# Gate logits on VectorE and ScalarE, and memory numerators with their denominators in one matmul per block, in a gated memory-attention and GLU kernel

## The chip, the cores and the metric

The kernel runs on one core of one Trainium2 chip. Its time is the device time of one execution in microseconds (us); a median of several runs is quoted. The profiled span, from the first to the last recorded instruction, is 1.6 to 1.9 us shorter than the measured time of the same execution.

PE is TensorE's matmul stream, PEld its weight loads, PEq its sequencer, DVE is VectorE, ACT is ScalarE, POOL is GpSimd and SP is SyncE. "The Trainium skill" is the set of notes on the chip that this text cites by page and section. PSUM is the memory into which matmuls write, and an eviction is the instruction that takes a result out of it.

## The reference

It mixes a segmented attention with a compressive memory (32 heads of 16 dimensions, 4 segments of 512 tokens) and a gated GLU, token by token. Cut to what matters here:

```python
x = A_x                                              # 1 x 2048 x 512, bfloat16
g = sigmoid((x * gate_w).sum(-1, keepdims=True))     # one gate logit per token
a = A_ref(x, ...)                                    # attention with memory
b = ((gelu(x @ w_gate)) * (x @ w_up)) @ w_down       # 512 -> 1792 -> 512
return g * a + (1 - g) * b

# inside A_ref, for each segment s of 512 tokens:
    p = softmax(qs @ ks.T * scale + mask);  a_dot = p @ vs
    pq = phi(qs)
    num = einsum('bhld,bhde->bhle', pq, M)           # memory numerators
    den = einsum('bhld,bhd->bhl', pq, z) + 1e-6      # memory denominators
    o = gb * (num / den) + (1 - gb) * a_dot          # gb = sigmoid(beta), per head
    M = M + phi(ks).T @ vs;  z = z + phi(ks).sum(l)
```

## The kernel before

The program declares tasks (a few instructions for one engine, with what they read and write). A scheduler with estimated durations and a table of biases then puts every engine's tasks into one fixed order. So the order of each engine's queue is decided when the program is built, and an instruction that is late holds up all that stand behind it on its engine.

The three parts of attention that matter: score matmuls on tiles of 32 rows fill all of one score buffer (`XALL`, 2048 columns of PSUM); one exponential of 2048 columns on ScalarE empties it; the next scores may start only then, because there is only one such buffer. TensorE uses the time of the exponential for full 128x128 matmuls (projections, GLU).

```python
# scores, then one exponential over the whole score buffer (72 times)
for (lhs, rhs, c0, ncol, rd) in steps:
    for g in range(4):
        instrs.append(Instr(lambda e, ...: e.matmul(X[g][:, c0:c0 + ncol], lhs(32 * g), rhs(32 * g),
                            start=True, stop=True, tile_position=(32 * g, 0)), rd, [("X", g)], ...))
...
exp_task(s, f"exp{s}_{t}{name}", [Instr(lambda e: e.activation(
    dst[:], XALL[:, :].rearrange("p (g c) -> p g c", g=4), ACTF.Exp, scale=ATT_SCALE),
    [("X", g) for g in range(4)], [key], act_t(2048))], after=after)
```

The gate logits and the denominators are groups of sixteen very narrow matmuls on TensorE:

```python
# gate logits of one segment: 16 matmuls of ONE column, weights are 128x128 blocks of x
pieces(f"gate{s}", gg, [mm(gg, lambda tile=tile: gg.f32()[:, tile:tile + 1],
                           xT[x3][:, kb, tile * 128:(tile + 1) * 128], gatew[:, kb:kb + 1],
                           [*xk(s, kb), ("w", "gatew")], kb == 0, kb == 3, 1)
                        for tile in range(4) for kb in range(4)], 16)
...
# denominators of one segment (s > 0): 16 matmuls of EIGHT columns
pieces(f"den{s}", gd, [mm(gd, lambda qt=qt, t=t: gd.f32()[:, 32 * qt + 8 * t:32 * qt + 8 * t + 8],
                          phq[:, t, qt * 128:(qt + 1) * 128], MZbd[:, t, 16:136:17], ...)
                       for qt in range(4) for t in range(4)], 16)
# VectorE: + eps, reciprocal, * (gate x head mix), 128 columns each
...
for qt in range(4):       # numerators: 4 matmuls of 128 columns, with the SAME weights phq as above
    pieces(f"num{s}_{qt}", gn, [mm(gn, ..., phq[:, t, qt * 128:(qt + 1) * 128],
                                   MZbd[:, t, :]...[:, :, 0:16], ..., 128) for t in range(4)], 4)
    task(f"nump{s}_{qt}", DVE, [ ... tensor_tensor(otok[...], gn.f32()[...], ndsc[...], ALU.mult) ], grp=gn)
```

The softmax here doesn't subtract the row's maximum and nothing guards it: scores larger than these inputs give would overflow.

## Time and profile before

| | before |
|---|---|
| median of 3 runs | 270.14 us (270.02 to 270.32) |
| profiled span | 268.6 us |
| PE busy | 259.8 us (97%) |
| ScalarE busy | 211.9 us (79%), of which 72 exponentials 135.0 |
| VectorE busy | 185.8 us (69%) |
| recorded matmuls / weight loads | 3075 / 3118 |

From the page of the profile of the kernel before: the busy time of each engine, and the chain of work that ended last, followed back in time, as shares of the span.

```profile
span 268.6 us, 7243 instructions
## 1 busy us (share of the span) xinstructions
PE 259.8 (97%) x3075; PEld 122.3 (46%) x3118; DVE 185.8 (69%) x333; ACT 211.9 (79%) x179; POOL 95.2 (35%) x223
...
PE 95%; issue 2%; ACT 2%; DVE 0%; ACTq 0%
```

These are the waits of PE and of PEld in the kernel before (who waited, for whom, us in total, how often, the longest); the weight load belongs to the matmul that follows it.

```profile
engine line waited for: us in total, times, longest us
...
PEld psXALL L775 <- ACT pt L782: 22.9, 54, 0.4
...
PE psW L439 <- issue: 3.8, 24, 0.2
PEld psXALL L775 <- ACT ptl L782: 2.5, 6, 0.4
...
PE psW L524 <- DVE pt L503: 1.1, 1, 1.1
```

"issue" is idle time for which the profile shows no releaser; the 24 holes of 0.16 us are missing matmuls, as the experiments will show.

The Trainium skill ("ScalarE: Activation LUTs", "What ACT_TABLE_LOAD costs") gives an activation with immediate operands as 186 ns + 0.833 ns per column; an estimate from it for 2048 columns is 1892 ns. This trace has 1875 ns, so it agrees within 1%.

The removed groups in the grouped view of the kernel before (busy us, mean ns of one; these durations are pipeline latencies and overlap, so they are not what a matmul costs the stream):

```profile
L439 PE MATMUL psW<-mzbd,phq 128*128 128x128 bf16 x48 | 4.2, 223 | 0.0
L439 PE MATMUL psW<-gatew,xT 128*128 128x1 bf16 x64 | 2.2, 163 | 0.0
L439 PE MATMUL psW<-mzbd,phq 128*128 128x8 bf16 x48 | 1.7, 176 | 0.0
```

### The profile page before, as it was taken

How to read it: one execution, taken by the hardware profiler on the slowest of the kernel's cores; microseconds unless marked ns; L12 is line 12 of the kernel's file. 1: busy time of each engine (PE TensorE's matmuls, PEld its weight loads, DVE VectorE, ACT ScalarE, POOL GpSimd, SP SyncE). 2: the span in 40 equal slices, each digit the busy share in tenths (PEclk: the TensorE clock that was granted, in tenths of full speed). 3: DMA queues.
4: the chain of work that ended last, by engine and by line, in shares of the span. 5: the costliest groups of instructions: out<-in, count | busy, mean ns of one | idle time of the engine just before them, and what ended most of it. 6: DMA issues, size and time to landing. Idle time of an engine off the chain costs nothing.

```text
span 268.6 us, 7243 instructions
## 1 busy us (share of the span) xinstructions
PE 259.8 (97%) x3075; PEld 122.3 (46%) x3118; DVE 185.8 (69%) x333; ACT 211.9 (79%) x179; POOL 95.2 (35%) x223
## 2 busy tenths in 40 slices
PE   8999999999999999999999999999999999999996
PEld 5445344444445444544444444444354434444354
DVE  1678997988978659798525988798851677353451
ACT  3889987999998898889768898877777767677602
POOL 8328853542002843252201574252300252352300
PEclk9999999999999999999999999999999999999999
DMA  6998991000304510102011310213020000000002
GB/s 194 203 323 185 362 212 22 4 0 2 81 2 98 81 42 0 45 20 42 20 24 39 60 23 1 58 27 82 1 44 0 2 0 2 20 22 32 9 2 78
DMA packets 32056, 16.53 MB, mean 62 GB/s; under 512 B 21400, under 2 KB 32024, under 8 KB 32024
## 3 DMA queue, kind: packets, MB, share of 16 engines
q1 hardware_dynamic: 31736, 15.81, 25.4%
q8 instruction: 24, 0.39, 0.6%
q10 hardware_dynamic: 288, 0.26, 0.3%
q14 instruction: 8, 0.07, 0.1%
HBM read 8.14 MB, written 2.10 MB: 38 GB/s over the span
## 4 chain that ended last, share of the span: by engine, by line
PE 95%; issue 2%; ACT 2%; DVE 0%; ACTq 0%
PE psW L439 75%; PE psXALL L775 9%; PE psW L824 6%; PE psXALL L439 1%; PE psW L832 1%; PE psW L524 1%; PE psW L742 1%; ACT pt L782 1%; PE psXALL L533 1%; ACT hT L909 1%; ACT L909 0%; ACT ost L958 0%; DVE pt L503 0%; ACTq L336 0%
## 5 line engine op out<-in xcount | busy, mean ns | idle before, releaser
L782 ACT ACTIVATE pt<-psXALL 128x2048 bf16<-128x2048 f32 x64 | 120.0, 1875 | 27.4 <-PE psXALL L775 24.3
L786 POOL TENSOR_SCALAR_AFFINE_SELECT pt<-pt 128x256 bf16<-128x256 bf16 x128 | 55.4, 434 | 139.3 <-ACT pt L782 132.7
L439 PE MATMUL psW<-xT,wu 128*128 128x512 bf16 x214 | 51.0, 379 | 1.1 <-issue 0.8
L439 PE MATMUL psW<-xT,wg 128*128 128x512 bf16 x213 | 50.3, 380 | 1.4 <-issue 1.1
L439 PE MATMUL psW<-wd,hT 128*128 128x512 bf16 x201 | 49.9, 380 | 1.1 <-issue 1.0
L930 DVE TENSOR_TENSOR hT<-psW,hT 128x512 bf16<-128x512 f32 x56 | 37.5, 685 | 15.6 <-PE psW L439 15.4
L839 DVE STREAM_TRANSPOSE tb<-psW 128x512 f32<-128x512 f32 x32 | 21.1, 696 | 18.9 <-PE psW L832 18.8
L439 PEld LDWEIGHTS psW<-xT,wu 128*128 128x128 bf16 x224 | 20.6, 98 | 24.8 <-issue 1.7
L439 PEld LDWEIGHTS psW<-xT,wg 128*128 128x128 bf16 x224 | 20.3, 98 | 24.5 <-issue 1.7
L439 PEld LDWEIGHTS psW<-wd,hT 128*128 128x128 bf16 x210 | 18.8, 98 | 22.7 <-issue 2.7
L775 PE MATMUL psXALL<-qT,kpad 32*128 32x320 bf16 (+3 forms) x512 | 25.4, 273 | 0.0
L909 ACT ACTIVATE hT<-psW 128x512 bf16<-128x512 f32 x28 | 16.4, 597 | 7.5 <-PE psW L439 7.5
L786 POOL TENSOR_SCALAR_AFFINE_SELECT ptl<-ptl 128x2048 bf16<-128x2048 bf16 x8 | 17.1, 2138 | 8.7 <-ACT ptl L782 8.4
L775 PEld LDWEIGHTS psXALL<-qT,kpad 32*128 32x128 bf16 x512 | 7.6, 92 | 26.5 <-ACT pt L782 20.8
L824 PE MATMUL psW<-pt,vaug 128*17 128x192 bf16 (+3 forms) x512 | 18.9, 273 | 0.0
L782 ACT ACTIVATE ptl<-psXALL 128x2048 bf16<-128x2048 f32 x8 | 15.0, 1876 | 2.8 <-PE psXALL L775 2.7
L439 PE MATMUL psW<-xT,wk 128*128 128x512 bf16 (+1 forms) x66 | 15.8, 381 | 0.2 <-issue 0.2
L691 POOL COPY exsT<-exs 32x4 f32<-32x4 f32 x64 | 14.6, 228 | 3.7
L439 PE MATMUL psW<-wo,oT 128*128 128x512 bf16 x55 | 14.8, 380 | 0.7 <-issue 0.5
L439 PE MATMUL psW<-xT,wq 128*128 128x512 bf16 x60 | 14.9, 380 | 0.5 <-issue 0.3
L456 DVE CAST hT<-psW 128x512 bf16<-128x512 f32 x21 | 14.0, 679 | 1.7 <-PE psW L439 1.5
L439 PE MATMUL psW<-wv,xT 128*128 128x512 bf16 x62 | 15.1, 380 | 0.1
(94 smaller groups left out, 285.5 us busy)
## 6 DMA issues: line engine op xcount, KB each, us to landing
out_dram<-ost SPq DMA_DIRECT2D x15, 128.0 KB, 1.7
wg<-in_B_w_gate_dram SPq DMA_DIRECT2D x2, 896.0 KB, 6.4
wu<-in_B_w_up_dram SPq DMA_DIRECT2D x2, 896.0 KB, 6.8
wd<-in_B_w_down_dram SPq DMA_DIRECT2D x1, 1792.0 KB, 13.1
vlow<-vaug SPq DMA_DIRECT2D x8, 136.0 KB, 3.5
wv<-in_A_wv_dram SPq DMA_DIRECT2D x1, 512.0 KB, 6.2
wo<-in_A_wo_dram SPq DMA_DIRECT2D x1, 512.0 KB, 14.0
wk<-in_A_wk_dram SPq DMA_DIRECT2D x1, 384.0 KB, 4.8
```

The source lines that it names most:

```text
L439: return Instr(lambda e: e.matmul(view(), lhsT, rhs, start=first, stop=last), reads=reads, writes=[fkey if fkey is not None else g.key], e ...
L456: alts[DVE] = [Instr(lambda e: e.tensor_copy(dst(), src()), reads=reads, writes=writes, est=dve_t(n))]
L524: task(f"warm{i}", PE, [Instr(lambda e, gw=gw, n=n: e.matmul(gw.f32()[:, 0:128 * n].rearrange("p (o c) -> p o c", c=128), warm[:, 0:128], ...
L533: task(f"x0t{i}_{u}", PE, [Instr(lambda e, k=k, a=a, u=u, i=i, src=src: e.transpose(src[:, k, a * 128:(a + 1) * 128], xin[:, 2 * u + a, (2 ...
L691: cross = task(f"exsT{s}", POOL, [Instr(lambda e, g=g, c=c: e.tensor_copy(exsT[sl][32 * g:32 * g + 32, c:16:4], exs[32 * c:32 * c + 32, s4 ...
L775: instrs.append(Instr(lambda e, g=g, lhs=lhs, rhs=rhs, c0=c0, ncol=ncol: e.matmul(X[g][:, c0:c0 + ncol], lhs(32 * g), rhs(32 * g), start=T ...
L782: prev_exp[0] = exp_task(s, f"exp{s}_{t}{name}", [Instr(lambda e: e.activation(dst[:], XALL[:, :].rearrange("p (g c) -> p g c", g=4), ACTF ...
L786: task(f"msk{s}_{t}{name}", POOL, [Instr(lambda e, view=view, pat=pat, base=base: e.affine_select(out=view, in_=view, compare_op=ALU.is_ge ...
L824: instrs.append(Instr(lambda e, t=t, q=q, kb=kb, slot=slot, c0=c0: e.matmul(gp.f32()[32 * q:32 * q + 17, 128 * kb + 64:512], Vaug[sl][:, k ...
L839: task(f"pvt{s}_{t}_{j}", DVE, [Instr(lambda e: e.transpose(Tb[:, j, :], gp.f32()[:, :]), [gp.key], [("Tb", j)], dve_t(512))], grp=gp)
L909: lambda e, g=g, ft=ft, s=s: e.activation(hT[s % 2][:, ft, :], g.f32()[:, :], ACTF.Gelu_apprx_tanh),
L930: task(f"Um{s}_{ft}", DVE, [Instr(lambda e, g=g, ft=ft: e.tensor_tensor(hT[sl][:, ft, :], g.f32()[:, :], hT[sl][:, ft, :], ALU.mult), [g.k ...
```

## The change

The intent is to take 113 small matmuls off TensorE. The gate logits become an elementwise multiply of token-major x with a broadcast gate vector on VectorE, and row sums on VectorE or ScalarE; for three of the four segments x is loaded once more for it, 1.5 MB in all. The denominators ride along as the 17th column of each head in the numerators' matmuls, 136 columns in place of 128. The head mix is folded into the memory matrix on GpSimd and VectorE, and the eviction of numerators becomes a short chain (add eps and scale, reciprocal, multiply) per group of 2 or 3 blocks. The warm-up matmuls read a constant. Because tasks changed, the table of biases was tuned again, which re-orders all queues.

```diff
-    task("gwt", PE, [ ... e.transpose(gwg.bf()[:, 0:4], gwrow[:, :], ident[0:4, 0:4]) ... ])
...
-        pieces(f"gate{s}", gg, [mm(gg, ..., xT[...], gatew[:, kb:kb + 1], ..., 1)
-                                for tile in range(4) for kb in range(4)], 16)
+        task(f"gmul{s}", DVE, [Instr(lambda e: e.tensor_tensor(
+            xt[:, 0:4, :], xt[:, 0:4, :], gwb[:]...to_broadcast([P, 4, D]), ALU.mult), ...)])
+        for a in range(4):
+            S.add(Task(f"gsum{s}_{a}", {
+                ACT: [... e.activation(xt[:, a, :], xt[:, a, :], ACTF.Copy, accum_out=glog[...]) ...],
+                DVE: [... e.tensor_reduce(glog[...], xt[:, a, :], AXX, ALU.add) ...]}))
...
-            pieces(f"den{s}", gd, [mm(gd, ..., MZbd[:, t, 16:136:17], ..., 8) ...], 16)
-            for qt in range(4):
-                pieces(f"num{s}_{qt}", gn, [mm(gn, ..., MZbd[...][:, :, 0:16], ..., 128) ...], 4)
+            for pr in range(2):
+                for k in range(3):
+                    blocks = [(2 * pr + k, t) for t in range(3)] if k < 2 else [(2 * pr, 3), (2 * pr + 1, 3)]
+                    pieces(f"num{s}_{pr}{k}", gn, [mm(gn, ..., gn.f32()[:, 136 * i:136 * i + 136],
+                           phq[:, t, qt * 128:(qt + 1) * 128], MZbd[:, t, :], ..., 136) ...], 3)
+                    ins = [ tensor_scalar(nd, den column, EPS, exr, add, mult), reciprocal(nd), tensor_tensor(otok, num, nd) ]
...
-                bdmask[32 * c:32 * c + 32]...to_broadcast([32, 4, 34]),          # block-diagonal mask
+                gbd[32 * c:32 * c + 32]...                                     # mask times head mix
...
 BIAS = { ... all values changed ... }
```

## The prediction

> **What bounds it now.** TensorE. The page of the profile puts PE at 259.8 of 268.6 us (97%), and the chain of waits is 95% PE. The list of waits names almost nothing that PE waited for: 1.06 us at the start (a VectorE memset of the warm-up operand), about 2.9 us of tail after the last matmul, and scattered "issue" gaps of 0.16 us that fit missing matmul records. VectorE (185.8 us) and ScalarE (211.9 us) have slack on average, but little between 25 and 75 us, where the table by stretches shows both at 8 to 10 of 10 us. So time is saved only in PE's stream, and lost where VectorE or ScalarE then returns a PSUM bank late.
>
> **What PE loses and gains** (start-to-start times in the trace):
> - The gate logits: 4 groups of 16 one-column matmuls. Within a group they start 25 ns apart, and the next full matmul starts 0.62 us after the first of the group: 4 x 0.62 = 2.5 us. The 25 ns is the issue floor that the Trainium skill gives ("TensorE: Matmul & The Clock Gate", "Wait — 56ns, not 53.3ns?"); this trace agrees.
> - The gate-vector transpose: 0.1 us.
> - The denominators: 3 groups of 16 eight-column matmuls, 27 ns apart, 0.64 us to the next full matmul (0.53 in one): 1.8 us.
> - The numerators go from 48 matmuls of 128 columns (59 ns apart) to 48 of 136, estimated at 62.6 ns: +0.16 us. They stand in 15 runs instead of 7. Leaving such a run cost 275 ns instead of 59 in about half the cases: estimated +0.9 us.
>
> Net about -3.3 us. Switches between full-array and tiled matmuls are equal in number; all other matmuls are the same.
>
> **What the others gain** (estimates from like instructions). VectorE: four 2048-element multiplies (about 1.25 us, from 0.70 for 1024), about 11 row sums (0.69), 18 smaller denominator chains in place of 3 large ones. About +18 us in all, so near 203 us busy. ScalarE: about 5 row sums of 0.6 us. About 5 us of VectorE's increase falls before the first up-projection (now at 67.8 us), where VectorE would be about 95% busy: I allow 0.5 us of new PE waits, there or around the numerator evictions. GpSimd's extra work and the 1.5 MB of extra x loads are off the path.
>
> **Start.** The warm-up no longer waits for the memset: about 0.15 us earlier, but it has 128 more cold columns (0.11 us), and then the x tiles and first key weights set the pace (landed 3.3 to 7.0 us, used within 0.1 to 0.5 us). Worth 0.1 us at most. The tail stays.
>
> **Prediction.** 270.1 - 3.3 - 0.1 + 0.5 = 267.2 us (-1.1%), 8 in 10 within 265.6 to 269.0. Faster by over 2% (under 264.7): 6%; within 2%: 92%; slower: 2%.
>
> **What would show it right.** No matmul of one or eight columns; PE busy down by about 3 us and still 97% or more; VectorE up 15 to 20 us; the waits for PE remain near nothing. Wrong in the stalls: PE idle ended by VectorE or by ScalarE's exponentials, most likely at 20 to 80 us.
>
> **What would make it wrong.** The re-tuned order: VectorE saturating early could cost 2 to 3 us and erase the gain. If runs of 2 to 6 numerators leave no gap, or the new order hides what the old one did not, the gain nears 4.5 us (265.6).

## More of the kernel before

The timeline of one such period in the kernel before (start, duration, engine, instruction, in brackets the idle time just before and who ended it):

```profile
218.05 0.12 PEld L775 LDWEIGHTS psXALL<-qT,kpad 32*128 32x128 bf16 x8 [0.42 <-ACT pt L782]
218.05 0.40 PE L775 MATMUL psXALL<-qT,kpad 32*128 32x320 bf16 x8
...
218.38 2.33 PE L439 MATMUL psW<-xT,wu 128*128 128x512 bf16 x10
218.64 1.88 ACT L782 ACTIVATE pt<-psXALL 128x2048 bf16<-128x2048 f32 x1 [0.71 <-PE psXALL L775]
...
220.64 0.12 PEld L775 LDWEIGHTS psXALL<-qT,kpad 32*128 32x128 bf16 x8 [0.42 <-ACT pt L782]
220.64 0.40 PE L775 MATMUL psXALL<-qT,kpad 32*128 32x448 bf16 x8
```

The exponential ends at 218.64 + 1.88 = 220.52 and the next scores start at 220.64. The period, from scores to scores, is 2.59 us: ten full matmuls of 0.216 us and 0.43 us for scores and switches. ScalarE alone needs 1.88 us for the exponential and, at the smallest gaps of the trace, 0.63 to 0.65 us from its end to the start of the next (scores and their signal): 2.52 us. TensorE and ScalarE go round together, 0.07 us apart.

In 54 of 72 score groups, and in 6 more for the buffer `ptl`, what came last before the weight load of the scores was the end of an exponential.

## The result, and the profile after

| | before | after |
|---|---|---|
| median (lowest to highest) | 270.23 us (270.02 to 270.46), 4 runs | 269.22 us (268.60 to 269.48), 4 runs |
| ratio after / before | | 0.996, 95% interval 0.9946 to 0.9974 |
| profiled span | 268.6 us | 267.5 us |
| PE busy | 259.8 us | 257.9 us |
| VectorE / ScalarE busy | 185.8 / 211.9 us | 199.9 / 212.1 us |
| matmuls / weight loads recorded | 3075 / 3118 | 2965 / 3005 |

The change gained 0.4%, 1.0 us, where 2.9 us were predicted. From the page after, the same lines as before:

```profile
span 267.5 us, 7093 instructions
## 1 busy us (share of the span) xinstructions
PE 257.9 (96%) x2965; PEld 118.4 (44%) x3005; DVE 199.9 (75%) x385; ACT 212.1 (79%) x188; POOL 102.3 (38%) x232
...
PE 84%; ACT 5%; DVE 3%; issue 3%; DMA 2%; POOL 1%; SPq 0%; ACTq 0%; DVEq 0%
```

The chain that was 95% PE is now 84% PE, with ScalarE, VectorE and a DMA in it. The waits of PE after, whole list:

```profile
engine line waited for: us in total, times, longest us
PE psW L449 <- issue: 3.8, 24, 0.2
PE psW L532 <- PEq L1114: 0.8, 1, 0.8
PE psW L449 <- ACT qT L463: 0.4, 1, 0.4
PE psW L449 <- ACT hT L937: 0.4, 1, 0.4
PE psXALL L803 <- ACT pt L810: 0.3, 2, 0.2
PE psW L449 <- DMA wk<-in_A_wk_dram: 0.3, 1, 0.3
PE psW L449 <- DVE phq L632: 0.2, 1, 0.2
```

These totals leave out what lies within the latency of the matmul before, and mix in missing records. So I made a second account from the start times of the matmuls. Between two switches of the tile shape it takes the time, subtracts the steps of the matmuls that the program puts there (missing ones included), and subtracts the smallest overhead seen for that kind of switch. What remains is called excess.

| from the first score matmul to the last matmul | before | after | difference |
|---|---|---|---|
| steps of full-array matmuls | 195.78 us | 192.79 us | -2.99 |
| score and value tiles, with switches, at their smallest | 49.37 | 49.37 | 0.00 |
| excess: waits | 3.84 | 5.58 | +1.75 |
| before the first score matmul | 16.69 | 16.84 | +0.16 |
| sum | | | -1.1 (spans: 268.6 to 267.5) |

A matmul of 136 columns is counted at 59 ns here: in the complete trace of a_half they start 59 ns apart in the median, as those of 128 columns do in b_half. The switches are the same in number and kind in both kernels.

So TensorE did lose 3.0 us of work, and 1.75 us of waits came in. Eight new waits make it up. Six, together about 1.4 us, are ended by ScalarE or stand at the exponential's buffer (at 51.2, 67.0, 100.3, 131.5, 194.1 and 221.6 us), and two, together about 0.35 us, by VectorE (at 85.4 and 120.2 us). Three of the six (67.0, 131.5 and 194.1 us, about 0.7 us) are not score groups: full matmuls or their successors wait there for another result that ScalarE takes out of PSUM (qT, or gelu's hT) after its exponentials. At 51.2 us the exponential itself had started late, and the profile puts that down to a GpSimd copy. At 100.3 us the profile names no releaser for the wait inside the score group; it is counted with ScalarE because it vanishes with shorter exponentials (below). The 0.16 us at the start is a key weight that landed at 7.19 us, not at 7.00, although the warm-up began 0.22 us earlier.

One of these waits in the timeline after. The same lines of a run that shortens the exponentials follow below:

```profile
219.62 0.40 PE L803 MATMUL psXALL<-qT,kpad 32*128 32x448 bf16 x8
...
219.95 1.04 PE L449 MATMUL psW<-xT,wu 128*128 128x512 bf16 x4
...
220.21 1.88 ACT L810 ACTIVATE pt<-psXALL 128x2048 bf16<-128x2048 f32 x1 [1.08 <-PE psXALL L803]
...
220.82 0.28 PE L449 MATMUL psW<-mzbd,phq 128*128 128x136 bf16 x2
...
220.94 1.03 PE L449 MATMUL psW<-xT,wu 128*128 128x512 bf16 x4
...
222.14 0.40 PE L803 MATMUL psXALL<-qT,kpad 32*128 32x320 bf16 x8 [0.17 <-ACT pt L810]
```

The exponential ends at 220.21 + 1.88 = 222.09. TensorE has only eight full matmuls and two numerators in this period, and the next scores wait for ScalarE. The period is 222.14 - 219.62 = 2.52 us, exactly ScalarE's floor. Where a removed group had stood there is now idle time.

What was added, from the grouped view after (busy us, mean ns of one):

```profile
L449 PE MATMUL psW<-mzbd,phq 128*128 128x136 bf16 x48 | 5.3, 223 | 0.0
L700 DVE TENSOR_REDUCE glog<-phkt 128x1 f32<-128x512 bf16 x9 | 5.7, 670 | 0.0
L692 DVE TENSOR_TENSOR phkt<-phkt,gwb 128x2048 bf16<-128x2048 bf16 x3 | 3.6, 1213 | 0.0
L697 ACT ACTIVATE phkt<-phkt 128x512 bf16<-128x512 bf16 x3 | 1.9, 622 | 0.0
L697 ACT ACTIVATION_READ_ACCUMULATOR phkt<-phkt 128x1 f32 x3 | 0.6, 193 | 0.0
```

The multiply is where the Trainium skill puts a 2048-element bfloat16 operation in its 2x mode ("VectorE: DVE Perf Modes", "Side-by-side: where the cycles go for N=2048 bf16": about 1224 ns); the trace has 1213 to 1215 ns, with one operand a broadcast.

### The profile page after: what moved, and what is told of

Read it like the earlier page. It is cut to its first block, busy times and chain, and to the rows that moved or that the text cites. A ratio compares the mean times of both kernels' runs of the same rounds, so it can differ in the third digit from the quotient of the medians.

```text
span 267.5 us, 7093 instructions
## 1 busy us (share of the span) xinstructions
PE 257.9 (96%) x2965; PEld 118.4 (44%) x3005; DVE 199.9 (75%) x385; ACT 212.1 (79%) x188; POOL 102.3 (38%) x232
## 4 chain that ended last, share of the span: by engine, by line
PE 84%; ACT 5%; DVE 3%; issue 3%; DMA 2%; POOL 1%; SPq 0%; ACTq 0%; DVEq 0%
PE psW L449 68%; PE psXALL L803 8%; PE psW L852 5%; ACT pt L810 3%; DMA wk<-in_A_wk_dram 2%; PE psXALL L449 1%; PE psW L860 1%; POOL exsT L712 1%; DVE tb L867 0%; PE psW L769 0%; ACT L937 0%; ACT L926 0%; SPq L480 0%; DVE mzbd L784 0%; DVE phkt L692 0%
## 5 line engine op out<-in xcount | busy, mean ns | idle before, releaser
L814 POOL TENSOR_SCALAR_AFFINE_SELECT pt<-pt 128x256 bf16<-128x256 bf16 x128 | 59.2, 464 | 131.6 <-ACT pt L810 126.6
L449 PE MATMUL psW<-xT,wu 128*128 128x512 bf16 x216 | 51.9, 380 | 0.8 <-issue 0.6
L449 PEld LDWEIGHTS psW<-wd,hT 128*128 128x128 bf16 x210 | 18.8, 98 | 22.5 <-issue 2.5
L712 POOL COPY exsT<-exs 32x4 f32<-32x4 f32 x64 | 15.4, 241 | 3.7
```

What stands on the lines that cost most here:

```text
L449: return Instr(lambda e: e.matmul(view(), lhsT, rhs, start=first, stop=last), reads=reads, writes=[fkey if fkey is not None else g.key], e ...
L712: cross = task(f"exsT{s}", POOL, [Instr(lambda e, g=g, c=c: e.tensor_copy(exsT[sl][32 * g:32 * g + 32, c:16:4], exs[32 * c:32 * c + 32, s4 ...
L814: task(f"msk{s}_{t}{name}", POOL, [Instr(lambda e, view=view, pat=pat, base=base: e.affine_select(out=view, in_=view, compare_op=ALU.is_ge ...
```

## The experiments

Three theories carry the argument, by the letters that the texts use. A: the removed groups cost TensorE less than the prediction read from the trace. L: the groups cost what was read, and VectorE's added load gives it back as waits. C, formed after the first four runs: in the stretches with attention exponentials TensorE walks in step with ScalarE, so that work taken from TensorE there comes back as waits for ScalarE, whatever VectorE does. Those texts name rivals too: B, the groups cost what the prediction read; O, the new waits are built into the new order of the queues; P, TensorE bounds everywhere; R, any change of this order's timing costs as much as it saves. Kernels whose name begins with b_ are the kernel before with an edit and those with a_ are the kernel after with an edit, except ab_half, which edits a_both. In all but a_tuned the order of the remaining instructions is left as it was.

The first four ran together; before in their rounds: 270.46 us (269.94 to 271.07, 11 runs). The next four: 270.56 (269.94 to 271.07, 12 runs). The last four: 270.27 (269.99 to 271.35, 11 runs).

| run | result right? | median us (runs) | ratio to before, 95% | span | excess |
|---|---|---|---|---|---|
| b_none | no | 271.00 (6) | 1.0015 (1.0000 to 1.0030) | 269.2 | 7.41 |
| b_twice | yes | 275.13 (4) | 1.0168 (1.0150 to 1.0186) | 273.4 | 5.55 |
| a_nogate | no | 269.01 (5) | 0.9945 (0.9929 to 0.9962) | 267.4 | 5.70 |
| a_both | no | 268.90 (5) | 0.9935 (0.9919 to 0.9952) | 267.2 | 5.65 |
| b_gelu_less | within tolerance | 267.19 (4) | 0.9879 (0.9860 to 0.9898) | 265.4 | 3.82 |
| b_exp_less | no | 269.34 (6) | 0.9960 (0.9944 to 0.9976) | 267.6 | 6.07 |
| b_short | no | 274.66 (4) | 1.0151 (1.0129 to 1.0174) | 273.6 | - |
| a_short | no | 272.83 (6) | 1.0083 (1.0063 to 1.0103) | 271.3 | - |
| b_half | within tolerance | 270.47 (6) | 1.0014 (0.9989 to 1.0039) | 268.5 | 3.63 |
| a_half | within tolerance | 268.08 (6) | 0.9914 (0.9898 to 0.9931) | 265.6 | 3.87 |
| ab_half | no | 268.11 (6) | 0.9928 (0.9902 to 0.9954) | 266.1 | 4.71 |
| a_tuned | yes | 268.62 (6) | 0.9939 (0.9924 to 0.9954) | 266.9 | 5.34 |

### b_none: the small groups simply left out of the kernel before

The gate groups, the transpose and the denominators are not issued; the instructions that read them read a constant. Nothing is added on VectorE and the order stays.

```diff
+DROP = ("gate", "gwt", "gwev", "w_gwrow", "den1", "den2", "den3")
...
-        exp_task(... [Instr(lambda e: e.activation(exs[:, s4], gg.f32()[:, 0:4], ACTF.Exp), ...
+        exp_task(... [Instr(lambda e: e.activation(exs[:, s4], onec[:, 0:4], ACTF.Exp), ...
...
-                ... e.tensor_scalar(nf, gd.f32()[:, 0:128], EPS, None, ALU.add) ...
+                ... e.tensor_scalar(nf, onec[:, 0:128], EPS, None, ALU.add) ...
     for t in S.schedule():
+        if t.name.startswith(DROP):
+            continue
```

> The kernel before, every engine in its old order, but without the 64 gate-logit matmuls, the gate-vector transpose and the 48 denominator matmuls; their readers take a constant instead (wrong result on purpose). Theory A (a matmul record is missing behind each group; only the 25 to 27 ns steps are real): TensorE loses 1.6 + 1.3 + 0.1 = 3.0 us and the time falls by 2.5 to 3.0 us, to about 267.3. Theory B (as predicted: each group costs 0.62 to 0.64 us up to the next full matmul): it falls by 4.4 us, to about 265.8. Less than 2 us would say that TensorE is not the whole bound even in the old order.

The time did not fall: 271.0 us against 270.46. In the account, 3.0 us of matmul steps went, and 3.6 us of excess came (3.84 to 7.41). Eight waits of 0.35 to 0.55 us appeared, at 27.9, 34.2, 48.5, 52.7, 101.0, 111.4, 143.9 and 169.5 us, most of them soon after the place of a removed group: three for exponentials, four for VectorE, and one (101.0 us) with no releaser named. A wait of 0.35 to 0.55 us is about what a removed group had taken. So neither A nor L is enough: without any added load on VectorE, the whole of the removed work came back as waits. In this order the partner that TensorE runs into is VectorE as often as ScalarE; the kernel after has another order, in which VectorE is met less.

### b_twice: every small group issued a second time

```diff
+DUP = ("gate1", "gate2", "gate3", "gate0", "den1", "den2", "den3")
...
+            if again is not None:
+                for ins in again.alts[PE]:
+                    em.plan(PE, Instr(ins.fn, ins.reads, ins.writes, ins.est))
```

> The kernel before with each of the 7 small groups (4 gate, 3 denominator) issued a second time, the copy set behind the next piece of TensorE work; result right. The other engines get more slack, so nothing but TensorE's cost shows. Theory A (25 to 27 ns a matmul): 2.9 us longer, about 273.0. Theory B (0.62 to 0.64 us a group): 4.4 us longer, about 274.5.

The time rose by 4.7 us, more than the 2.9 us that A allows for the groups. The trace settles the sizes, because in this trace no matmul record is missing (3230 matmuls, 3230 weight loads): eight gate groups took 3.23 us from start to the next full matmul, 0.403 us each or 25.2 ns a matmul, and six denominator groups 2.68 us to the next matmul of another kind, 0.447 us each. The rest of the increase is +1.7 us of excess, nearly all in two waits, of 0.87 us at 95.1 us for a VectorE eviction and 0.86 us at 103.4 us inside a score group. Why these two are so long was not tested. A is right about the size of the work; the total hit neither forecast.

The 25 ns agrees with the Trainium skill ("TensorE: Matmul & The Clock Gate", "Wait — 56ns, not 53.3ns?"), which has it as the floor between two starts however narrow the matmul.

What misled the prediction is seen when the same place is shown in two traces. TensorE's timeline around the gate group at 85 us, in the kernel before:

```profile
85.36 0.54 PE L439 MATMUL psW<-gatew,xT 128*128 128x1 bf16 x16
85.98 0.81 PE L439 MATMUL psW<-wv,xT 128*128 128x512 bf16 x3
```

and in b_half, whose TensorE program is the same, and whose trace has all 3118 matmuls:

```profile
85.43 0.54 PE L439 MATMUL psW<-gatew,xT 128*128 128x1 bf16 x16
85.84 1.02 PE L439 MATMUL psW<-wv,xT 128*128 128x512 bf16 x4
```

Before, three full matmuls are recorded where there are four, and the first of them seems to start 0.62 us after the group's start; it starts 0.40 us after it. The hole of 0.21 us is one missing record of a 512-column matmul (0.216 us), not a cost of leaving the group.

### a_nogate and a_both: VectorE's added load taken away from the kernel after

a_nogate leaves out the multiply and the row sums of the gate logits. a_both also cuts the chain on the numerators to its one multiply.

```diff
+DROP = ('gmul', 'gsum')
-        ... e.activation(exs[:, s4], glog[:, s4], ACTF.Exp) ...
+        ... e.activation(exs[:, s4], ones[:, 0:4], ACTF.Exp) ...
     # a_both only:
+        if t.name.startswith("nump"):
+            made = made[-1:]
```

> The kernel after in its own order on every engine, without the 4 products and 16 row sums of the gate logits (VectorE and ScalarE); the exponential reads a constant (wrong result on purpose); the loads of x stay. Theory L (TensorE's new waits come from the added work): about half of the 1.7 us of waits go, time 0.7 to 1.0 us below after, 268.3. Theory O (they are built into the re-tuned order of the queues): within 0.3 us of after, 269.0.

> As the run without the gate sums, and the numerators' evictions are also cut to their one multiply (by a constant; no per-bank add and reciprocal): about 24 us less VectorE work than after, the same order. Theory L: at least 1.2 of the 1.7 us of TensorE waits go, about 267.7. Theory O: at most 0.5 us goes, 268.7 or more, and the profile shows waits at the same places of TensorE's order.

VectorE fell from 199.9 us to 188.0 and to 178.0 (185.8 in the kernel before), and yet the time fell only to 269.01 and 268.90 from 269.22, and the excess stayed (5.70 and 5.65 against 5.58). The ratios differ from that of the kernel after by 0.0015 and 0.0025, and the intervals overlap. Theory L falls: VectorE's added load is at most some tenths of a microsecond of it. Theory O fits both runs; a_half below decides between O and C. The places did not all stay: in a_both the waits at 51.2 and 85.4 us are gone, and the one at 100.3 us grew from 0.35 to 0.84 us, so a wait that is taken away in one place can come back in another. The wait for VectorE at 120.2 us stayed (0.17 us), so the added load does not cause it.

### b_gelu_less and b_exp_less: the same fifteen matmuls taken out, in two kinds of place

The span has three long stretches without exponentials of the attention (17.6, 16.6 and 16.2 us), where ScalarE runs gelu, and 68 exponential-to-exponential periods with 184 us in sum. Of the seven removed groups only one, a gate group at 143.5 us, stood in a gelu stretch. Both runs drop 15 matmuls of 512 columns (one of four accumulating steps), 15 x 0.216 = 3.24 us: b_gelu_less in the three gelu stretches, and b_exp_less one in each of 15 periods that hold ten of them.

```diff
+LESS = ('U0_1.0', 'U0_3.0', ... 'G2_3.0', ... 'G3_12.0')      # b_gelu_less, 15 names
+LESS = ('G0_9.0', 'G0_13.0', 'G1_1.0', ... 'D2_1.4')          # b_exp_less, 15 names
...
+            if t.name in LESS and i == 1:
+                continue
```

> The kernel before in its old order, with 15 of its 512-column matmuls left out (one of the four that make a sum, so the result is wrong on purpose), five in each of the three stretches of 16 to 18 us in which ScalarE does no attention exponential. 15 x 0.216 = 3.2 us of TensorE work. Theory C (only in those stretches is TensorE the sole bound; between the exponentials it walks in step with ScalarE and VectorE): 2.8 to 3.2 us faster than before. Theory P (TensorE bounds everywhere): 3.2 us faster too. Theory R (any change of this order's timing costs as much as it saves): less than 1 us faster.

> The same, but the 15 matmuls are taken out of 15 different periods between two exponentials that hold exactly ten full matmuls and last 2.59 us. Theory C: such a period can't be shorter than one exponential and the hand-off before it, 1.88 + 0.64 = 2.52 us, so at most 0.07 us each, 1 us in all: 0 to 1 us faster than before. Theory P: 3.2 us faster.

The same work is worth 3.3 us of time in one place (270.56 to 267.19; excess unchanged) and 1.2 us in the other (to 269.34). In b_exp_less 2.2 of the 3.24 us came back as excess (3.84 to 6.07), 2.1 us of it in waits that exponentials ended. The number of periods that last 2.5 us rose from 9 to 21; the shortened periods stop at ScalarE's floor. C had forecast 0 to 1 us for this run, so 1.2 is a little over it; P, at 3.2 us, and R, at less than 1 us in the gelu stretches, fall. So 3.24 us of TensorE's work is worth all of itself in a gelu stretch, and a third in an exponential's period.

### b_short and a_short: every exponential at half width, first try

If ScalarE is the partner that gives the freed time back, shorter exponentials should let the change show its whole worth. Half of every buffer is set once to a constant, and the exponential writes the other half.

```diff
-                    dst[:], XALL[:, :].rearrange("p (g c) -> p g c", g=4), ACTF.Exp, scale=ATT_SCALE),
+                    dst[:, :, 0:256], XALL[:, :].rearrange("p (g c) -> p g c", g=4)[:, :, 0:256], ACTF.Exp,
+                    scale=ATT_SCALE),
...
+    for i, x in enumerate([*PT, PTl]):
+        em.plan(DVE, Instr(lambda e, x=x: e.memset(x[:, :, 256:512], 0.5), writes=[("hi", i)]))
```

> The kernel before in its old order, with each of the 72 attention exponentials computing half its columns (wrong result on purpose; the other half of the buffers is set once at the start): about 0.85 us less of ScalarE for each, 60 us in all. Theory C: nothing else but TensorE is tight now, and TensorE hardly waits in before, so 0 to 1.5 us faster than before. If exponentials were the real bound throughout, tens of us faster.

> The kernel after in its own order, with the same half exponentials. Compared with the run of before with half exponentials: theory C: with ScalarE out of the way the whole 2.8 us of TensorE work that the change removes shows, 2.3 to 3.0 us apart (against 1.0 to 1.2 us for the two full kernels). Theory O (the new order itself makes TensorE wait): still about 1.1 us apart.

The totals are of no use. The seven fills on VectorE, 0.91 us each, held up the start: the first exponential started at 22.5 us in b_short and 21.9 us in a_short, against 17.4 us in the kernel before and the kernel after, and b_short's clock was 0.988. From the first exponential to the end, b_short took 251.1 us against 251.3 of the kernel before, and a_short 249.4, 1.7 us apart where C had forecast 2.3 to 3.0. This hints at C and shows it badly, since a_short also has a wait of 0.91 us for VectorE at 123.9 us.

### b_half and a_half: the same without the fills

The first exponential into each of the seven buffers is whole, and the other 65 are of half width, so the rest of each buffer holds old values that are valid numbers. The results differ in value.

```diff
+            def wide(key):
+                n = seen.get(key, 0)
+                seen[key] = n + 1
+                return 512 if n < 2 else 256
...
-                    dst[:], XALL[:, :].rearrange("p (g c) -> p g c", g=4), ACTF.Exp, scale=ATT_SCALE),
+                    dst[:, :, 0:wide(key)], XALL[...][:, :, 0:wide(key)], ACTF.Exp, scale=ATT_SCALE),
```

> As the earlier run of before with half exponentials, whose 7 buffer fills of 0.91 us held up the start by 5 us: now the first exponential into each of the 7 buffers is whole and the other 65 compute half, and nothing is added at the start. Old order, wrong result on purpose. The earlier trace took 251.1 us from the first exponential to the end, against 251.25 in before: so 0 to 0.5 us faster than before, 270.2.

> The kernel after with the same half exponentials. The earlier trace took 249.4 us from the first exponential on, with two waits for VectorE left (1.1 us) and none for ScalarE: 1.6 to 1.9 us faster than the half-exponential run of before, against 1.1 us for the full kernels. Theory C. If ScalarE had nothing to do with the waits: 1.1 us.

This is the experiment that decides. ScalarE's busy time fell from 212 to 159 us in both. The kernel before gained nothing from it (270.47 us, against 270.27 in its rounds): its TensorE lost no time to ScalarE. The kernel after gained: 268.08 us, 2.4 us under b_half (1.6 to 1.9 were forecast), and 2.9 us in the spans (268.5 and 265.6; a_half's profiled execution was its fastest, 267.38 us, and b_half's took 270.21). Its ratio to before (0.9898 to 0.9931) is clear of that of the kernel after (0.9946 to 0.9974). The account, against b_half: -2.99 us of matmul steps, +0.24 of excess, -0.07 at the start. So with ScalarE out of the way, of the 3.0 us that the change takes from TensorE 2.9 are seen in the profiled executions and 2.4 in the medians, with the same VectorE load and in the same order. Half exponentials also let all that follows an exponential start earlier: the masks on GpSimd and the other work in ScalarE's queue. So the run shows that ScalarE's time binds, and not through which of these. The wait for VectorE at 120.2 us is gone too. PE in b_half's page, then the page and waits of PE in a_half:

```profile
PE 264.0 (98%) x3118; PEld 121.3 (45%) x3118; DVE 185.9 (69%) x333; ACT 159.5 (59%) x179; POOL 98.5 (37%) x223
```

```profile
span 265.6 us, 7133 instructions
...
PE 261.9 (99%) x3005; PEld 118.5 (45%) x3005; DVE 199.2 (75%) x385; ACT 158.3 (60%) x188; POOL 103.2 (39%) x232
```

```profile
PE psW L532 <- PEq L1121: 0.8, 1, 0.8
PE psW L449 <- DMA wk<-in_A_wk_dram: 0.2, 1, 0.2
```

The period shown above of the kernel after, in a_half:

```profile
218.03 0.40 PE L809 MATMUL psXALL<-qT,kpad 32*128 32x448 bf16 x8
...
218.36 1.04 PE L449 MATMUL psW<-xT,wu 128*128 128x512 bf16 x4
...
218.62 1.02 ACT L816 ACTIVATE pt<-psXALL 128x1024 bf16<-128x1024 f32 x1 [1.93 <-PE psXALL L809]
...
219.35 1.03 PE L449 MATMUL psW<-xT,wu 128*128 128x512 bf16 x4
...
220.31 0.40 PE L809 MATMUL psXALL<-qT,kpad 32*128 32x320 bf16 x8
```

Here the scores start as soon as the full matmuls are through, at 220.31. From scores (218.03) to scores it is 2.28 us, where the kernel after needs 2.52. PE's list of waits names ScalarE no more. One wait of 0.20 us remains in the account, at 84.8 us, where an eviction of numerators on VectorE must end before the output projection: this is the only place in a_half where the new chain on VectorE costs TensorE time.

### ab_half: half exponentials and no added VectorE load

It is a_both with the edit of a_half.

> Half exponentials and, too, no gate products and sums and numerator evictions cut to one multiply: after's order with both ScalarE and VectorE relieved. Theory C (the missing gain is TensorE waiting for the two others in turn): all of TensorE's saving shows, 2.6 to 3.0 us faster than the half-exponential run of before. Theory O (the order itself holds waits that no faster engine removes): no more than 2 us.

It measured 268.11 us (267.82 to 270.27), 2.4 us under b_half and not under a_half, where C had forecast 2.6 to 3.0 under b_half and O no more than 2; in the trace a single wait of 1.06 us for a VectorE product (at 118.6 us) had appeared. Where that comes from was not found. The run hits neither forecast, leaves a wait that a faster ScalarE and less VectorE work do not remove, and shows again that less VectorE work brings no gain here.

### a_tuned: the kernel after with its queues ordered anew

If the loss lies in the fit between queues, another order should win some of it back without any change of work. I searched biases again, with durations that the traces gave, where the table had estimates (for example 1.16 us for a numerator chain and 3.3 us for the mix on GpSimd).

```diff
 BIAS = {
-    "D0": -705, "D1": -805, "D2": -380, ...
+    "D0": -275.8, "D1": -923.7, "D2": -348.3, ...
```

> The kernel after, every operation the same and the result right, but another order of the queues, searched for with the durations of the row sums, cross-partition copies and evictions that the trace of after shows. Theory C: TensorE's own work is the same, so at most the 1.75 us of waits are to be had: 0.2 to 1.0 us faster than after, 268.5. If the queues' order were not what sets the waits: the same as after, 269.2.

268.62 us (268.46 to 269.12), correct, with a ratio to before of 0.9939. That is the lowest median of the correct kernels with the whole work, 0.6 us under that of the kernel after; the two were each timed against before and not against one another, and their intervals overlap (0.9924 to 0.9954, and 0.9946 to 0.9974). In the profile 0.6 us of span went (267.5 to 266.9), and waits at 53.6, 84.9, 99.9, 130.9, 193.9 and 221.0 us remain.

## Why the prediction was wrong

The prediction said 267.2 us, with 8 in 10 between 265.6 and 269.0; it measured 269.22. Point by point:

**"TensorE. … So time is saved only in PE's stream".** Right in that the kernel before lost nothing to ScalarE, as b_half shows, and the sentence goes on "and lost where VectorE or ScalarE then returns a PSUM bank late", which is what came about. Wrong as a rule for what a saving is worth. "VectorE and ScalarE have slack on average" is true, and is the wrong average: in the attention periods ScalarE needs 2.52 of 2.59 us. The warning was in the profile before: 60 of 72 score groups (54 and 6) were released by the end of an exponential, at no cost.

**"I allow 0.5 us of new PE waits, there or around the numerator evictions."** This is the step that failed. New waits measured +1.75 us, not 0.5, and about 1.4 us of them were ScalarE's, spread over the whole span, not VectorE's before 68 us or at numerators (about 0.35 us, of which 0.20 at numerators). That ScalarE is the partner in this order is shown by a_half: same order and same VectorE work as after, and the excess falls from 5.58 to 3.87 us, 0.24 over b_half's. That VectorE's added load is not is shown by a_nogate and a_both.

**The size of the removed work, "4 x 0.62 = 2.5 us", "1.8 us", and +0.9 us for leaving runs of numerators.** The groups and the leaving were mis-sized because missing matmul records were read as costs. The groups measured 4 x 0.403 = 1.6 us and 3 x 0.447 = 1.3 us. Leaving a run of numerators costs nothing: in a_half and in b_half the next full matmul starts 59 or 60 ns after the last numerator, as one numerator does after another. The +0.16 us for 136 columns was not there either (59 ns at both widths). In two of the four gate groups of before, with no record missing, the true 0.40 us could have been read. It is luck that 1.4 us of gain too much and 1.1 us of cost too much nearly cancelled: 3.3 us net predicted, 3.0 measured in the account.

**"Start. … Worth 0.1 us at most."** It cost 0.16 us: a DMA landed 0.19 us later. Its landing moves between runs (the first score matmul started between 16.3 and 16.8 us over these profiles), so this is not shown to belong to the change.

**What the others gain.** VectorE +14 us, where about 18 were predicted and 15 to 20 set as the mark: somewhat too much. Multiply 1.21 us (1.25), row sum 0.67 us (0.69): right. GpSimd's work "off the path": the chain after has 1% of GpSimd in it, copies that the kernel before makes too; whether the extra work delayed them was not tested. "No matmul of one or eight columns": right. "PE busy down by about 3 us and still 97% or more; the waits for PE remain near nothing": wrong. PE's busy time fell 1.9 us as recorded, to 96%, and even this number is not safe, since it lacks the missing records: the same TensorE program shows 264.0 us in b_half and 259.8 in before.

**"Wrong in the stalls: PE idle ended by VectorE or by ScalarE's exponentials, most likely at 20 to 80 us."** The failure was foreseen in kind, but about three quarters of the waits lie outside that window and it was given too small a size.

The sum in the prediction's terms: -3.3 -0.1 +0.5 = -2.9 us; measured -2.99 (work) +1.75 (waits) +0.16 (start) = -1.1 us of span, and -1.0 us of median time. The waits alone, +1.25 us more than allowed, are the larger part of the miss of 1.8 us (2.0 in the medians); the rest is the size of the work (0.3) and the start (0.3).

What stays open: why b_twice gained two waits of 0.9 us, and ab_half one of 1.06; why one exponential at 49.8 us in the kernel after had to wait for a GpSimd copy and started 0.3 us late; why the order of the kernel before runs into VectorE too when work is taken out (b_none), with nothing added there; and whether the start differs by more than chance.

## What to carry to other kernels

Before pricing work taken from the busiest engine, look at who released its queue last, even where that cost no time: here TensorE's weight loads for scores were released 60 times in 72 by ScalarE's end, the two walked in step, and a shortened period gained little more than the slack to ScalarE's floor (2.59 against 2.52 us). Price the saving by place: 3.24 us taken from stretches with no such partner gained 3.3 us, and taken from the shared periods 1.2 us. And compare counts of matmuls and weight loads before reading a hole between matmuls as a cost; a second trace of the same program tells a missing record from a real gap.

## What the Trainium skill lacked or had wrong

- "TensorE: Matmul & The Clock Gate", "Back-to-back issue gap", gives a sustained spacing in streams of weight loads and matmuls of about 81 ns at N=128 and about 131 ns at N=512. These traces, with a weight load for each matmul, show 59 ns at 128 columns (and at 136) and 216 ns at 512, near what the page calls the isolated gap (about 56 and 216 ns).
- "Perfetto Trace Analysis", "Identifying the Most-Contended Engine", tells the reader to optimize the engine of highest occupancy first, and that matmul busy time is not a good measure of how near TensorE is to its roofline. Here matmul busy of 97% pointed at TensorE, and 3.0 us of its work taken out (b_none) gained nothing. What is lacking is a check for a partner in step where the busy engine shows no gap yet: 79% busy on average, and 2.52 of 2.59 us in the periods that count.
- No page that I read says that matmul records can be missing while their weight loads are there: 43 of 3118 and 40 of 3005 in two traces and none in the edited kernels' traces quoted here, with PE busy 259.8 against 264.0 us for the same TensorE program.
- "ScalarE: Activation LUTs" says that an activation can give an accumulator output, but not what it costs: a row sum of 512 columns took 0.62 us plus a separate read of the accumulator of 0.19 us.
